# Full attention layers in runs of three score tiles, with one exponential tile of a quad on VectorE

## The chip, the cores and the metric

The kernel runs on one core of a Trainium2 chip. The metric is the device time of one execution in microseconds (us). The engines are named as in the profile: PE (TensorE, matmuls), PEld (its weight loads), DVE (VectorE), ACT (ScalarE), POOL (GpSimd) and SP (the engine whose queue issues the DMAs).

## The reference

Four transformer attention layers on one sequence of S = 2048 tokens and D = 512 features, with 32 heads of 16 features each. Layers 0 and 2 look back over a sliding window of 256 tokens, layers 1 and 3 attend to all 2048 tokens in both directions.

```python
q, k, v = split_heads(layernorm(x) @ wqkv)          # 32 heads of 16
scores = einsum("bhqd,bhkd->bhqk", q, k) * 16 ** -0.5
# layers 0, 2: positions outside 0 <= i - j < 256 are masked
p = softmax(scores)
x = x + merge_heads(einsum("bhqk,bhkd->bhqd", p, v)) @ wo
# x = x + A(x); x = x + B(x); x = x + A(x); x = x + B(x)   (A: window, B: full; weights shared)
```

In a full layer each head has 2048 x 2048 scores, all of which need an exponential.

## The kernel before

**Quads.** In a full layer the unit of work is a quad: four heads (two pairs) against one block of 512 queries. There are 8 quads of heads and 4 query blocks `c`, so 32 quads in a layer. Layer 1 goes through them block by block; layer 3 takes two quads of one feature tile `t` for each block in turn, 16 such blocks of two quads. A quad runs over 16 tiles `j` of 128 keys. For each `j` and each of the two pairs PE multiplies keys with queries (line 714, two matmuls of 64 rows side by side, one for each head) into a score tile of 128 keys by 2 x 512 queries in PSUM, and ACT writes its exponential to SBUF in float32 (line 718). So a quad has 32 score tiles and 32 exponentials. The values of one `j` are four float32 matmuls, one for each head (line 758; the profile shows two passes of each, eight records), which add up over the 16 `j` in the PSUM tile `acc[0]`, a quarter of the partitions for each head. A column of ones in the values adds up the denominator. Behind the last `j` the epilogue (lines 681 to 703) transposes `acc[0]` on DVE, divides by the denominator and writes the result as two float16 parts.

**PSUM.** In the full layers the eight banks hold `acc[0]`, `acc[1]` and three score tiles of two banks each: two of a rotating pool and `PH["third"]`. Every third score tile takes the third, so tile number k always uses the place of tile k - 3.

**Order on PE.** PE executes in the order in which the program is written; the other engines' orders are made by the framework from the priorities (`tc.high_priority(HEAD_START)` moves an instruction ahead). In `attn_full` one step is one `j`: both pairs' scores, then the values of the `j` two steps earlier (`pvq`, `flush(2)`), then side work.

**Side work** is everything that the neighbouring layers need: projections to queries, keys and values, the output projection and the layer norm behind it. It is cut into pieces of one matmul of 512 columns, which in full layers is issued as four matmuls of 32 columns abreast (`mms`, line 429), all into the bank `acc[1]`. A bank takes 12 pieces (3 in layer 3's output projection), and DVE then empties it; the planner lets 1.6 or 2.2 us of its own clock pass before it starts the next one (`PH["free"]`). `Side.share` hands out pieces against a budget; `Side.finish` issues what is left at the end of a stretch with no attention in between. `MM` is the planner's cost of one piece, 0.222 us.

**Loads.** `load_full` fetches a quad's queries (256 KB) and its keys in two halves (512 KB each) over SP's queue. There are three key buffers and two query buffers. The next quad's load is written at the start of the present one, but not over the end of a block.

Of the kernel before, what the change touches and what calls it, by code (L numbers as in the profile page):

```python
# [19 lines left out]
P = 128  # L20
# [13 lines left out]
EB, XB, XNB, WB, VB, OB = 6, 4, 4, 2, 3, 5  # L34
L_MIN = 2.0 ** -90
# [151 lines left out]
def fast_path(ctx, tc, flag, a_x, a_wqkv, a_wo, b_wqkv, b_wo, out):  # L187
# [20 lines left out]
    XC, XN, V, O, OT, KM, PH = {}, {}, {}, {}, {}, {}, {"free": 0.0}  # L208
    CM, DN, DC, WT, ST, pend = {}, {}, {}, {}, {}, []

# [287 lines left out]
    def project(l, s, c, act, ht=None, first=None):  # L498
# [14 lines left out]
        for t in range(NHT) if ht is None else (ht,):  # L513
# [9 lines left out]
            with tc.high_priority(HEAD_START):  # L523
# [33 lines left out]
    def keys(l, c, act, ht=None, first=None):  # L557
        sqs = yield from project(l, 1, c, act, ht, first)

        def rest():  # L560
# [4 lines left out]
            with tc.high_priority(HEAD_START):  # L565
                nc.vector.tensor_reduce(KM[l][r, c:c + 1], ph[r], axis=AX.X, op=ALU.max)  # L566
# [74 lines left out]
    def wo(l, c, tail):  # L641
# [4 lines left out]
        for i in range(4):  # L646
# [4 lines left out]
            with tc.high_priority(HEAD_START):  # L651
                nc.vector.tensor_tensor(d, ps, gcol[l % 2], ALU.mult)
# [25 lines left out]
    def epilogue(l, c, qd, a):  # L678
# [6 lines left out]
        with tc.high_priority(HEAD_START if l % 2 else 0):  # L685
            nc.vector.transpose(ot.rearrange("p b r -> p (b r)"), a)  # L686
# [19 lines left out]
    def exps(name, kt, qt, pr, pieces):  # L706

        turn["s"] += 1
        ps = PH["third"] if PH["full"] and turn["s"] % 3 == 0 else ps_s.tile([P, 2, QC], F32, name=f"s{name}", tag="s")
        w0 = min(p[3] for p in pieces)  # L710
        w1 = max(p[3] + p[2] for p in pieces)
# [5 lines left out]
        e = pp.tile([P, 2, QC], F32, name=f"e{name}", tag="e", bufs=EB)  # L717
        nc.scalar.activation(e[:, :, w0:w1], ps[:, :, w0:w1], AF.Exp, scale=SCALE)  # L718
        return e
# [30 lines left out]
    def attn_full(l, c, qd, kt, qt, a):  # L750
        for j in range(NT):
            es_ = []
            for pr in range(2):
                es_.append(exps(f"{l}_{c}_{qd}_{j}_{pr}", kt[j // 8], qt, pr, [(j % 8 * P, 0, QC, 0)]))

            def pv(j=j, es_=es_):
                for h in range(4):
                    nc.tensor.matmul(a[32 * h:32 * h + DH + 1, :], V[l, qd // 4, j // 8][:, j % 8, 4 * (qd % 4) + h, :],  # L758
                                     es_[h // 2][:, h % 2, :], start=(j == 0), stop=(j == NT - 1),
                                     skip_group_check=True)  # L760
            yield pv
# [5 lines left out]
    def attn_win(l, c, qd, kt, qt, a):  # L767
        first = True
        for u, tiles in enumerate(WTILES):
            tiles = [p for p in tiles if c or p[0] >= 0]  # L770
            es_ = []
            for pr in range(2):
# [4 lines left out]
                for b, far in edges:  # L777
                    v = ev[:, :, b, :]
                    with tc.high_priority(HEAD_START):
# [80 lines left out]
    class Side:  # L860

        def __init__(self, steps, works=(), following=(), least=0.0):
            self.next, self.least = list(following), least
            self.q, self.steps, self.cost, self.spent, self.k = [], steps, 0.0, 0.0, 0
            self.budget = self.lag = 0.0
# [10 lines left out]
        def one(self, force=False):  # L876

            if force:
                self.prefetch()
            at = [(w.ready_at(), i) for i, w in enumerate(self.q)]  # L880
# [11 lines left out]
        def piece(self, w):  # L892
# [4 lines left out]
            self.spent += abs(c)  # L897
            return c
# [9 lines left out]
        def step(self):  # L908
# [7 lines left out]
            if PH["full"]:  # L916
                return self.share()
# [6 lines left out]
        def share(self):  # L924

            self.budget = min(self.budget + max((self.cost - self.spent) / max(self.steps - 3 - self.k, 1), self.least), 0.75)
            self.lag = max(self.lag - max(0.29, self.least), -0.3)
            while self.q and clock[0] >= PH["free"] and self.budget >= MM / 2 and (self.lag < 0.25 or self.budget > 0.45):
# [4 lines left out]
                self.lag += abs(c)  # L933
# [21 lines left out]
    def attention(l, works):  # L955

        win = l % 2 == 0
        phase(l)
        load = load_win if win else load_full
        sd = None  # L960
        for t in range(NHT if l == 3 else 1):
            for c in range(NQ):
                qds = range(2 * t, 2 * t + 2) if l == 3 else range(NQD)
                if l == 1:

                    sd = sd or Side(NT * NQD // 2, works[0], works[1], 0.33)
                    while ("Q", 1, c) not in DONE:
                        sd.one(True)
                    settle()
                else:  # L970
                    sd = Side((3 if win else NT) * len(qds), works[t * NQ + c], works[t * NQ + c + 1], 0.34 if l == 3 and t < 2 else 0.0)
# [223 lines left out]
```

## Time and profile before

| | |
|---|---|
| median of 3 runs | 2768.49 us (2767.56 to 2770.2) |
| profiled execution | 2767.5 us, its span 2765.8 us |
| mean granted clock of PE | 0.992 |
| PE, ACT, DVE, POOL busy | 95%, 86%, 35%, 21% |
| layer 0 and what comes before it | 0 to 506 us |
| layer 1 (full) | 506 to 1458 us |
| layer 2 and its neighbours | 1458 to 1792 us |
| layer 3 (full) | 1792 to 2748 us |

The bounds of the layers are the first and last exponentials of each, as the trace has them. A row of the profile gives the line, the engine, the operation and its operands, then the count; matmuls are pipelined, so the length of one is more than the distance from one to the next. In the full layers ACT's instructions overlap too: one starts before the one ahead of it has ended, so distances between starts or ends tell more than durations.

### The profile page before, as it was taken

Reading aid. Unit: us, or ns where it says so; the run is one execution under the profiler, and the core shown is the slowest. Engines: PE = TensorE matmul, PEld = TensorE weight load, DVE = VectorE, ACT = ScalarE, POOL = GpSimd, SP = SyncE. Lnnn points to the kernel's source line nnn. Section 1 sums busy time; section 2 is a strip of 40 time slices with the busy share of each in tenths; the row PEclk is TensorE's granted clock in tenths of the full one; section 3 lists DMA queues with packets and bytes.
Section 4 is the critical chain, followed back from the end, with each engine's and each line's share of the span. In section 5 each row is a group of like instructions: output and inputs, shape, how many; then the busy total and the mean of one; then the engine's idle time right before and its main releaser. Section 6 shows DMA issues by size and latency. Waiting matters only on the chain.

```text
span 2765.8 us, 59954 instructions
## 1 busy us (share of the span) xinstructions
PE 2629.3 (95%) x24502; PEld 779.9 (28%) x24502; DVE 959.7 (35%) x2063; ACT 2377.9 (86%) x2683; POOL 567.7 (21%) x1129
## 2 busy tenths in 40 slices
PE   8989989999999999999998888899999999999997
PEld 4333334322222222222223333422222222222221
DVE  7678765112131113112215676512222222222122
ACT  3666655799999999999995677399999999999997
POOL 2577662000000000000005677100000000000000
PEclk9999999999999999999999999999999999999999
DMA  7877775422232123212325564623333343333331
GB/s 225 224 244 227 224 202 161 139 70 89 85 100 88 63 81 108 85 60 91 101 68 177 149 186 133 177 66 112 105 117 116 120 124 104 102 107 114 99 96 56
DMA packets 318542, 345.32 MB, mean 125 GB/s; under 512 B 113072, under 2 KB 234416, under 8 KB 312240
## 3 DMA queue, kind: packets, MB, share of 16 engines
q1 hardware_dynamic: 318256, 341.39, 41.0%
q8 instruction: 194, 3.18, 0.5%
q14 instruction: 92, 0.75, 0.1%
HBM read 228.59 MB, written 96.99 MB: 118 GB/s over the span
## 4 chain that ended last, share of the span: by engine, by line
PE 74%; ACT 8%; issue 6%; DVE 6%; POOL 3%; DMA 3%; SPq 0%; ACTq 0%; DVEq 0%; POOLq 0%
PE acc L758 30%; PE s L714 19%; PE acc L429 10%; PE b L432 9%; ACT e L718 7%; PE acc L791 3%; PE bs L432 1%; POOL e L781 1%; POOL e L784 1%; DVE ot L686 1%; POOL wr L344 1%; DMA w<-wd 1%; DVE xh L469 1%; DVE sp L528 0%; DVE xn L463 0%
## 5 line engine op out<-in xcount | busy, mean ns | idle before, releaser
L718 ACT ACTIVATE e<-s 128x1024 f32<-128x1024 f32 (+2 forms) x2432 | 2245.6, 1115 | 106.4 <-PE s L714 98.4
L758 PE MATMUL acc<-e,vt 128*17 128x512 f32 x8192 | 1078.8, 598 | 4.9 <-DVE ot L686 4.1
L714 PE MATMUL s<-qt,kt 64*128 64x512 f16 (+3 forms) x5504 | 777.8, 355 | 68.2 <-ACT e L718 40.0
L714 PEld LDWEIGHTS <-kt 64*128 64x128 f16 x5504 | 203.1, 94 | 807.4 <-issue 776.0
L784 POOL TENSOR_SCALAR_AFFINE_SELECT e<-e 128x256 f32<-128x256 f32 x512 | 230.4, 457 | 116.0 <-ACT e L718 115.3
L758 PEld LDWEIGHTS acc<-e,vt 128*17 128x17 f32 x8192 | 136.2, 95 | 383.6 <-issue 351.8
L686 DVE STREAM_TRANSPOSE ot<-acc 128x512 f32<-128x512 f32 x128 | 91.3, 714 | 374.6 <-PE acc L758 308.5
L781 POOL TENSOR_SCALAR_AFFINE_SELECT e<-e 128x256 f32<-128x256 f32 x448 | 196.8, 445 | 91.0 <-ACT e L718 89.5
L702 POOL TENSOR_TENSOR oh<-o,oh 128x512 f16<-128x512 f32 x31 | 36.0, 1161 | 860.2 <-DVE oh L701 860.2
L791 PE MATMUL acc<-e,vt 128*17 128x384 f32 (+2 forms) x2816 | 202.0, 393 | 6.1 <-POOL e L781 4.0
L432 PE MATMUL b<-xc,w 128*128 128x512 f16 x684 | 159.4, 384 | 16.8 <-DMA w<-wd 7.8
L533 POOL TENSOR_TENSOR sq_h<-sp_h 128x512 bf16<-128x512 f16 x27 | 28.1, 1041 | 510.8 <-DVE sp_h L527 510.8
L525 ACT ACTIVATE sp<-b,es 128x512 f16<-128x512 f32 x57 | 39.2, 688 | 96.0 <-PE b L432 93.7
L527 DVE TENSOR_SCALAR sp<-acc,es 128x512 f16<-128x512 f32 x28 | 20.9, 748 | 288.9 <-PE acc L429 288.9
L638 DVE COPY vt<-acc 128x256 f32<-128x256 f32 (+1 forms) x40 | 20.2, 504 | 288.9 <-PE acc L429 288.9
L527 DVE TENSOR_SCALAR sp_h<-acc,es 128x512 f16<-128x512 f32 x27 | 20.3, 751 | 277.8 <-PE acc L429 277.1
L533 POOL TENSOR_TENSOR sq<-sp 128x512 bf16<-128x512 f16 x28 | 29.1, 1041 | 396.9 <-DVE sp L527 396.9
L429 PE MATMUL acc<-xc,w_h 128*32 128x512 f16 x1296 | 108.1, 379 | 2.3 <-DVE km L566 2.3
L429 PE MATMUL acc<-xc,w 128*32 128x512 f16 x1344 | 108.9, 379 | 0.3
L673 DVE TENSOR_TENSOR dx<-acc,gcol 128x512 f32<-128x512 f32 x60 | 41.5, 692 | 176.7 <-PE acc L429 176.7
L429 PE MATMUL acc<-wv,xc 128*32 128x256 f16 (+1 forms) x1920 | 101.7, 306 | 0.0
L429 PE MATMUL acc<-wo,oh 128*32 128x512 f16 x1296 | 101.3, 379 | 0.0
(167 smaller groups left out, 1767.0 us busy)
## 6 DMA issues: line engine op xcount, KB each, us to landing
kt<-kf SPq DMA_DIRECT2D x128, 512.0 KB
qt<-qs SPq DMA_DIRECT2D x128, 256.0 KB
xd<-x SPq DMA_DIRECT2D x96, 256.0 KB
x<-xd SPq DMA_DIRECT2D x96, 256.0 KB
w<-wd SPq DMA_DIRECT2D x20, 1024.0 KB
kt<-kw SPq DMA_DIRECT2D x64, 256.0 KB
qs<-sp SPq DMA_DIRECT2D x48, 256.0 KB
wo<-wd SPq DMA_DIRECT2D x12, 1024.0 KB
```

The lines of the kernel that those rows point to most:

```text
L429: nc.tensor.matmul(ps[g:g + 32], a[:, g:g + 32], b, start=(i == 0), stop=(i == len(pairs) - 1), skip_group_check=True)
L432: nc.tensor.matmul(ps, a, b, start=(i == 0), stop=(i == len(pairs) - 1))
L527: nc.vector.tensor_scalar(sp[:, 0], ps, e, None, op0=ALU.mult)
L533: nc.gpsimd.tensor_tensor(sq, sp[:, 0], sp[:, 0], ALU.mult)
L673: nc.vector.tensor_tensor(d, ps, gcol[1], ALU.mult)
L686: nc.vector.transpose(ot.rearrange("p b r -> p (b r)"), a)
L714: nc.tensor.matmul(ps[:, h, s0:s0 + wd_], kt[R * h:R * h + R, pr, kc:kc + P], qt[R * h:R * h + R, pr, qc:qc + wd_], start=True, stop=True)
L718: nc.scalar.activation(e[:, :, w0:w1], ps[:, :, w0:w1], AF.Exp, scale=SCALE)
L758: nc.tensor.matmul(a[32 * h:32 * h + DH + 1, :], V[l, qd // 4, j // 8][:, j % 8, 4 * (qd % 4) + h, :], es_[h // 2][:, h % 2, :], start=(j ...
L781: nc.gpsimd.affine_select(v, v, pattern=[[0, 2], [-1, P]], compare_op=ALU.is_gt, fill=0.0, base=0, channel_multiplier=1)
L784: nc.gpsimd.affine_select(v, v, pattern=[[0, 2], [1, P]], compare_op=ALU.is_ge, fill=0.0, base=0, channel_multiplier=-1)
L791: nc.tensor.matmul(a[32 * h:32 * h + DH + 1, q * P:(q + nb) * P], V[l, (4 * c + j) // 4][:, j % 4, 4 * qd + h, :], es_[h // 2][:, h % 2, s ...
```

## The change

Only the full layers change; the window layers keep their step and merely get a function of their own (`attention_win`).

**Runs of three.** `attention_full` counts score tiles over quad ends. After every third one, `run` emits on PE: the values that became ready in earlier runs (at most two `j`, and none behind an epilogue), then side work. What became ready in this run waits for the next one. So PE's order is three score tiles, one to two `j`'s values, side pieces. The room for side pieces in a run is 1.79 us less 0.87 for each `j` emitted, and at least one piece (two behind an epilogue). The budget holds up to six pieces; a bank that was begun is filled before other work is taken (`within`).

**One exponential on DVE.** In all quads of layer 3 and those of layer 1's first three query blocks, the second pair's tile at `j` = 1 is not given to ACT. `exps_vector` reads the scores from PSUM with one DVE instruction over 2 x 512 columns, and then for each of the two heads computes the exponential in 10 instructions over 512 columns (round to a power of two, a polynomial of degree 6, scale). The result lies in a buffer of its own, `EX`, which takes one of the three places of the window layers' values; the work that needs the last place waits for the start of layer 1's last block (`"X"`). The values of `j` = 1 are issued in two halves: the first pair's with the others, the second pair's behind those of `j` = 12.

**Loads.** The next quad's keys and queries are requested after a run in the second half of a quad, as soon as what they need is done, also across blocks.

**Priorities.** Evictions that had a head start of 100 instructions get 300 in full layers (`head()`).

```diff
+JX, LATE = 1, 11
+    head = lambda: 3 * HEAD_START if PH["full"] else HEAD_START
...
+    def exps_vector(ps):
+        with tc.high_priority(head()):
+            nc.vector.tensor_scalar(EX[0][:, 0], ps, -126.0 / (SCALE * LOG2E), SCALE * LOG2E, op0=ALU.max, op1=ALU.mult)
+        b, k2 = EX[0][:, 1, 0], EX[0][:, 1, 1]
+        for h in range(2):
+            a = EX[0][:, 0, h]
+            nc.vector.tensor_scalar(k2, a, MAGIC, None, op0=ALU.add)
+            nc.vector.scalar_tensor_tensor(a, k2, MAGIC, a, op0=ALU.subtract, op1=ALU.subtract)
+            nc.vector.tensor_scalar(k2.bitcast(I32), k2.bitcast(I32), 23, None, op0=ALU.logical_shift_left)
+            nc.vector.tensor_scalar(b, a, POLY[6], POLY[5], op0=ALU.mult, op1=ALU.add)
+            nc.vector.tensor_tensor(b, b, a, ALU.mult)
+            for k in range(4, 0, -1):
+                nc.vector.scalar_tensor_tensor(b, b, POLY[k], a, op0=ALU.add, op1=ALU.mult)
+            nc.vector.scalar_tensor_tensor(a, b, POLY[0], k2, op0=ALU.add, op1=ALU.mult)
+        return EX[0][:, 0]
...
+        def emit(all_=False):
+            n, over = 0, False
+            while due:
+                f = due[0]
+                if f.__name__ == "pv":
+                    if not all_ and (n + f.size > 2 or over):
+                        break
+                    n += f.size
+                else:
+                    over = True
+                due.popleft()()
+            return n, over
+
+        def run():
+            nonlocal pairs, began
+            pairs = 0
+            spent(0.22)
+            n, over = emit()
+            due.extend(ready)
+            ready.clear()
+            sd.step(max(1.79 - 0.87 * n, 2 * MM if over else MM))
+            clock[0] = began = max(clock[0], began + 2.71)
...
+            vector = l == 3 or c < NQ - 1
...
+            for j in range(NT):
+                es_ = []
+                for pr in range(2):
...
+                    if vector and j == JX and pr:
+                        es_.append(exps_vector(scores(n, *piece)))
+                        ready.append(values_of(l, c, qd, j, es_, (0,)))
+                        held = values_of(l, c, qd, j, es_, (1,))
+                    else:
+                        es_.append(exps(n, *piece))
+                        if pr:
+                            ready.append(values_of(l, c, qd, j, es_))
+                    if pr:
+                        if vector and j == JX + LATE:
+                            ready.append(held)
+                        if j == NT - 1:
+                            ready.append(lambda c=c, qd=qd: epilogue(l, c, qd, acc[0]))
+                    pairs += 1
+                    if pairs == 3:
+                        run()
+                        if j >= NT // 2 and not ops and i + 1 < len(quads) and all(d in DONE for d in upcoming(i + 1)):
+                            settle(False)
+                            if not pend:
+                                ops = load_full(l, *quads[i + 1][1:])
```

167 lines of the change are left out of this document (99 added, 68 removed).

## The prediction

> **What bounds the kernel now.** I read the page first, then the two full layers (the parts of the change) by line, by wait and in order of time. The sum is made against the profiled execution: span 2765.8 us, its time 2767.5 us, 1.0 us under the median of 2768.49.
>
> ```profile
> span 2765.8 us, 59954 instructions
> PE 2629.3 (95%) x24502; PEld 779.9 (28%) x24502; DVE 959.7 (35%) x2063; ACT 2377.9 (86%) x2683; POOL 567.7 (21%) x1129
> PE 74%; ACT 8%; issue 6%; DVE 6%; POOL 3%; DMA 3%; SPq 0%; ACTq 0%; DVEq 0%; POOLq 0%
> ```
>
> The chain follows PE, but a busy PE is not a full one, so I asked how close ACT is to its own end in the full layers. Rows of the exponentials' line in layer 1 and in layer 3 (count, least/median/greatest ns, first and last start), and ACT alone in order of time (start, length, count):
>
> ```profile
> L718 ACT ACTIVATE e<-s x1024: 1017/1045/1590, 507.0 to 1456.8; 128x1024 f32<-128x1024 f32 x171
> L718 ACT ACTIVATE e<-s x1024: 1018/1124/1706, 1792.4 to 2745.8; 128x1024 f32<-128x1024 f32 x171
> 956.99 321.29 ACT L718 ACTIVATE e<-s 128x1024 f32<-128x1024 f32 x348 [0.28 <-PE s L714]
> 2499.62 247.93 ACT L718 ACTIVATE e<-s 128x1024 f32<-128x1024 f32 x270
> ```
>
> In the last row 270 tiles end within 247.93 us: (247.93 - 1.2 for the first)/269 = **0.917 us** a tile, with no gap; that is ACT's floor, although one tile takes 1.02 us from its start. A quad (32 tiles) can't go under 29.34 us there. Layer 1 takes 950.7 us (first start to last start and one tile), 29.7 a quad, layer 3 954.3, 29.8. Where side work is dense (third row) a tile takes 321.29/348 = 0.923. So both engines are near their limits, and all that a better order of PE can win is 0.4 us a quad.
>
> What PE does in a step of two tiles, dense (1004 to 1008) and nearly free of side work (2702 to 2704):
>
> ```profile
> 1004.73 1.05 PE L758 MATMUL acc<-e,vt 128*17 128x512 f32 x8
> 1005.60 0.61 PE L429 MATMUL acc<-xc,w 128*32 128x512 f16 x8
> 1006.14 0.61 PE L714 MATMUL s<-qt,kt 64*128 64x512 f16 x4
> 1006.68 1.05 PE L758 MATMUL acc<-e,vt 128*17 128x512 f32 x8
> 1007.55 0.40 PE L429 MATMUL acc<-xc,w 128*32 128x512 f16 x4
> 1007.88 0.61 PE L714 MATMUL s<-qt,kt 64*128 64x512 f16 x4
> ...
> 2002.68 0.38 PE L714 MATMUL s<-qt,kt 64*128 64x512 f16 x2
> 2002.99 1.05 PE L758 MATMUL acc<-e,vt 128*17 128x512 f32 x8
> ...
> 2702.98 1.05 PE L758 MATMUL acc<-e,vt 128*17 128x512 f32 x8
> 2703.96 0.92 PE L714 MATMUL s<-qt,kt 64*128 64x512 f16 x4
> ```
>
> From start to start: one tile's scores and the turn to the values 0.31 (2002.68 to 2002.99), two 0.54, so 0.23 for each tile ahead of the last; the values of one j 0.87; one side piece (four matmuls abreast) and the turn to the scores 0.33, two 0.54, so 0.21 for each further one; values straight to scores 0.98, that is 0.11 for the turn. A dense step is 0.54 + 0.87 + 0.33 or 0.54 = 1.74 or 1.95, on average 1.845 against ACT's 1.834: PE leads by a hair.
>
> How the two hand over:
>
> ```profile
> 506.50 0.66 ACT L636 ACTIVATE vt<-bs 128x256 f32<-128x256 f32 x2 [1.93 <-PE bs L432]
> 507.21 0.39 PE L714 MATMUL s<-qt,kt 64*128 64x512 f16 x2 [0.42 <-ACT vt L636]
> ...
> 2006.19 0.61 PE L714 MATMUL s<-qt,kt 64*128 64x512 f16 x4
> 2006.68 2.98 ACT L718 ACTIVATE e<-s 128x1024 f32<-128x1024 f32 x3 [1.42 <-PE s L714]
> ```
>
> A score matmul follows the end of the ACT operation that frees its bank by 0.05 us (507.16 to 507.21); an exponential follows its first score matmul by 0.49 (2006.19 to 2006.68).
>
> **The change, part by part.**
>
> *Runs of three.* There are three score buffers, and now PE writes all three in one go, then values, then side work. The third scores of a run (S3) need the third exponential of the run before to have ended. From S3's start the clock runs: that exponential ended 0.05 earlier and began 1.07 earlier; ACT took the run's first tile 0.917 after that, 0.15 before S3, and has work for 2.75 us, until S3 + 2.60. The next run's first scores must start 0.49 before that: **S3 + 2.10 us**. Now the step of two has 0.31 + 0.87 + 0.54 = 1.72 between its last scores and the next first ones, so it never meets this bound. In the run the distance depends on what it emits:
> - one j's values and four pieces: 0.31 + 0.87 + 0.33 + 3 x 0.21 = 2.14, 0.04 late;
> - two j's and one piece (the room given is at least one): 0.31 + 1.74 + 0.33 = 2.38, **0.28 late**; without a piece 0.31 + 1.74 + 0.11 = 2.16, 0.06 late.
>
> ACT can't earn this back: the run after a late one has PE early, but ACT still needs 2.75 for its three tiles. Three tiles make one j and a half, so one and two j's alternate; walking the queue of values through 32 quads by the code gives, for a quad, 4.3 runs with two j's, 2.0 with one and a half, 4.3 with one (5.3 and 5.3 without the vector tile). The saving is there too: three turns in 2.75 us in place of four and a half, some 0.1 a run of PE's time, but PE doesn't use it, since S3 waits.
>
> *The vector tile* (24 quads of layer 1, 32 of layer 3). ACT has 31 tiles, 28.43 us. But the j's values are cut in two halves, of two heads each. Is a half 0.44 or 0.87? The eight matmuls of a j (four heads, two passes) take 0.60 each and 1.05 together, so the four of a pass run abreast, and two would take as long:
>
> ```profile
> L758 PE MATMUL acc<-e,vt 128*17 128x512 f32 x4096 | 538.7, 598 | 3.8 <-DVE ot L686 3.2
> ```
>
> I take 0.87; the lower end is 0.44. Then both runs with one and a half j's, with the two pieces that they are given, are 0.31 + 1.74 + 0.54 = 2.59, 0.49 late (0.06 by the lower end). The vector tile's own run always has one j: in it ACT is done 0.92 early, at S3 + 1.18. With four pieces the next scores come at 2.14 all the same, so ACT idles through what it was spared; what remains is that the run of one and a half j's behind it isn't late on top. Without side work they come at 0.31 + 0.87 + 0.11 = 1.29, and 0.8 is won.
>
> A quad then: full of side work 29.34 + 4.3 x 0.28 + 0.49 = **31.0** (26 pieces); one piece a run 29.34 + 5.3 x 0.28 - 0.6 = 30.2 (11 pieces); none 29.34 + 5.3 x 0.06 - 0.8 = 28.9. Full and without a vector tile (layer 1's last eight) 29.34 + 5.3 x 0.28 = 30.8.
>
> *Side work.* Rows of the side matmuls in layer 1 (first four) and in layer 3:
>
> ```profile
> L429 PE MATMUL acc<-xc,w 128*32 128x512 f16 x1344 | 108.9, 379 | 0.3
> L429 PE MATMUL acc<-wo,oh 128*32 128x512 f16 x576 | 46.4, 379 | 0.0
> L429 PE MATMUL acc<-wv,xc 128*32 128x512 f16 x576 | 45.3, 379 | 0.0
> L429 PE MATMUL acc<-wv,xc 128*32 128x256 f16 x576 | 24.7, 273 | 0.0
> ...
> L429 PE MATMUL acc<-xc,w_h 128*32 128x512 f16 x1296 | 108.1, 379 | 2.3 <-DVE km L566 2.3
> L429 PE MATMUL acc<-wo,oh 128*32 128x512 f16 x720 | 54.9, 379 | 0.0
> L429 PE MATMUL acc<-wv,xc 128*32 128x256 f16 x768 | 31.7, 277 | 0.0
> ```
>
> By four, and the narrow ones by eight: 696 pieces in layer 1, 21.8 a quad; 600 in layer 3, 18.8. Between 30.2 and 31.0 that is 30.8 and 30.6; about one run in fourteen has none because a bank has just been filled (to 30.66 and 30.48). Layer 1: 32 x 30.66 = 981, **+30**. Layer 3: 32 x 30.48 = 975, **+21**. In layer 3's first half a block of two quads has 49 pieces and 21 runs at 2.2: walking its queue leaves two banks of the output projection for the forced end in seven blocks, six pieces (1.3 us) and one eviction between (1.2): 7 x 2.5 = **+17**, at least 0 if they fit.
>
> *Loads.* Keys and queries of the next quad are now issued in the second half of a quad, when their buffer is free, and over the ends of blocks. Stalls of this kind that cost PE now:
>
> ```profile
> PEld L714 <- DMA kt<-kf: 6.0, 1, 6.0
> ACT e L718 <- PE s L714: 13.5, 19, 6.0
> ```
>
> One, 6.0 us, at the head of layer 3, where nothing can be fetched ahead; of the other 7.5 us of ACT's waits there I take **-5** (0 to -7.5). SP's queue holds less behind a load that waits for its buffer; nothing on the path waits for that today.
>
> *DVE.* No 128x512 immediate operation stands in the trace; nearest rows:
>
> ```profile
> L653 DVE TENSOR_TENSOR x<-x,dx 128x512 f32<-128x512 f32 x12 | 8.8, 730 | 0.4
> L527 DVE TENSOR_SCALAR sp<-acc,es 128x512 f16<-128x512 f32 x28 | 20.9, 748 | 288.9 <-PE acc L429 288.9
> L463 DVE TENSOR_SCALAR xn<-x,mv,y 128x512 f32<-128x512 f32 x12 | 6.6, 548 | 0.3
> 1000.00:1050.00 50.00, 49.91 (x488) 11.68 (x488) 12.13 (x26) 49.93 (x55) 2.95 (x3) 1.00 0.27 91
> ```
>
> First operation on two banks at most 2 x 0.75 = 1.5, six with one input at 0.55, fourteen with two at 0.73: 15.0 us in one chain (13 if a one-input operation took half). It is wanted eight runs later, 8 x 2.8 = 22.4, in which DVE's other work (12.13 of 50) takes 5.4: 20.4, it fits. Evictions now wait up to one 0.7 us operation more; runs are 2.7 apart, so I take 0 for that, and up to +10.
>
> **Sum**: 2767.5 + 30 + 21 + 17 - 5 = 2830.5; **2830**. Lower ends: halves at 0.44 save about 0.4 in 56 quads, -22, no forced ends -17: 2791; upper: evictions +10, each run full +20: 2860. Likeliest case's own range 2791 to 2860.
>
> **The rivals.**
>
> *A, faster: the bound at S3 doesn't bind*, because the order in which PE's queue really runs lets the next first scores start under S3 + 2.10 in nearly all runs (it decides from 0.3 us a run). Then each engine runs at its own sum. PE, a quad: 10.67 x 0.77 + 17 x 0.87 + 21.8 x 0.21 + 10.67 x 0.12 = 28.9 in layer 1, 28.2 in layer 3; ACT 28.43. Layer 1: 24 x 28.9 + 8 x 29.34 = 928, -22; layer 3: 32 x 28.43 = 910, and some 8 of waits: -36. **2710**. For it: ACT's gapless 247.93 us; against it: three buffers and S3's place in the order. The Trainium skill (Perfetto Trace Analysis, Identifying the Most-Contended Engine) judges TensorE by its weight loads, not by its busy share, and takes the engine with the highest occupancy as the one to relieve: by that ACT bounds the full layers and PE, at 28% PEld, has room, so 56 tiles less would be 56 x 0.917 = 51 us off, near this case. The dense step of 1.845 against 1.834 speaks against it.
>
> *B, slower still: DVE is late.* If the chain interleaves with evictions and epilogues so that it ends 2 us behind its wanted run in a third of the quads, PE stands 18 x 2 = 37 us: **2867**. Against it: 20.4 of 22.4.
>
> *C, no change*: pieces fall mostly into the runs with one j, and the late runs just cancel what the vector tile spares: **2768**. Against it: the room is never under one piece.
>
> **How the numbers follow.** The forecast 0.52, A 0.33 (its partial forms with it), B 0.08, C 0.07. Range: 2710 to 2862 takes in A's upper half and B's lower edge and leaves out about 2 in 10. Faster by over 0.2% (5.5 us, about what a measurement here can tell from no change) 0.33, within 0.07, slower 0.60.
>
> **What would show it.** In the changed trace ACT would have a gap of 0.2 to 0.5 us behind most runs with two emissions of values, released by the scores; the third scores of a run would start 0.05 behind an ACT end; a half j's values would take 0.87. Layer 1 would last near 981 us and layer 3 near 987 with its ends. Wrong: if ACT's row stays unbroken at 0.917 a tile with 31 in a quad, or layer 1 is under 950 us.

## The result and the profile after

The change makes the kernel slower: **2917.38 us** in place of 2768.02 on the same chip, a ratio of **1.0539** (95% interval 1.0519 to 1.0559). The forecast was 2830, with 2862 as its upper end: the direction was right, and 87 us of the loss were missing.

The page of the changed kernel (span; busy time, share of the span and count of each engine; chain of waits by engine):

```profile
span 2911.3 us, 61028 instructions
PE 2656.0 (91%) x24502; PEld 875.1 (30%) x24502; DVE 1664.7 (57%) x3239; ACT 2355.0 (81%) x2627; POOL 577.6 (20%) x1129
PE 43%; ACT 14%; DVE 12%; issue 6%; DMA 1%; POOL 1%; SPq 0%; ACTq 0%; DVEq 0%
```

Before, PE held 74% of the chain and DVE 6%. Here the chain can be followed back only to 678 us (its shares add up to 77%), so the fair comparison is that stretch, 678 us to the end, in both kernels: PE had 78% of it and now has 56%, DVE had 54 us and now has 354, of which 224 are operations of the vector tile. So the chain now passes from PE to ACT and DVE and back. DVE's busy time grew by 705 us, while ACT was spared only 23 us. PE's busy time grew by 27 us with the same 24502 matmuls.

Where the time went, by stage, from the first to the last of the full layers' values matmuls in the trace: layer 1 949.5 to 1016.4 (+67), layer 3 951.9 to 1031.5 (+80), all between them 336.4 to 337.3. So the whole loss lies in the two full layers. ACT's exponentials there (count, busy, mean ns, idle time ahead of them and what ended it), first layer 1 and then layer 3 of the changed kernel:

```profile
L720 ACT ACTIVATE e<-s 128x1024 f32<-128x1024 f32 x1000 | 938.4, 1035 | 67.3 <-PE s L728 62.4 <-PE acc L784 4.5
...
L720 ACT ACTIVATE e<-s 128x1024 f32<-128x1024 f32 x992 | 933.1, 1033 | 106.9 <-PE s L728 88.4 <-PE acc L784 17.9
```

And the same two rows of the kernel before:

```profile
L718 ACT ACTIVATE e<-s 128x1024 f32<-128x1024 f32 x1024 | 947.1, 1084 | 3.7 <-PE s L714 2.7
...
L718 ACT ACTIVATE e<-s 128x1024 f32<-128x1024 f32 x1024 | 946.7, 1199 | 14.4 <-PE s L714 13.5
```

Idle time of 3.7 and 14.4 us has become 67.3 and 106.9. ACT now stands idle until score matmuls are there, and the score matmuls stand until ACT has freed a bank: each holds the other up. The waits of the whole run (waiter, releaser, us in total, times, longest):

```profile
ACT e L720 <- PE s L728: 246.1, 386, 15.0
PE s L728 <- ACT e L720: 131.3, 334, 1.4
PEld L558 <- DVE sp_h L536: 15.7, 12, 3.8
PE acc L437 <- DVE vt L646: 14.6, 14, 2.0
PE acc L437 <- DVE dx L681: 10.5, 17, 0.9
PE acc L558 <- POOL sq_h L541: 9.3, 6, 3.1
```

These sums hold the window layers too. In the two full layers alone the first row is 77.4 and 88.4 us (5.6 and 13.5 before), the second 44.7 and 46.5 (0.5 and 0.3 before). The last four rows are side work: matmuls that wait for a bank that DVE has not emptied, or for what GpSimd makes from it.

One pair of runs in order of time (start, length, count, idle time ahead):

```profile
991.78 0.82 PE L728 MATMUL s<-qt,kt 64*128 64x512 f16 x6
992.27 5.60 ACT L720 ACTIVATE e<-s 128x1024 f32<-128x1024 f32 x6 [0.98 <-PE s L728]
992.53 1.05 PE L784 MATMUL acc<-e,vt 128*17 128x512 f32 x8
993.40 1.04 PE L437 MATMUL acc<-xc,w 128*32 128x512 f16 x16
...
994.38 0.61 PE L728 MATMUL s<-qt,kt 64*128 64x512 f16 x4
995.18 0.39 PE L728 MATMUL s<-qt,kt 64*128 64x512 f16 x2 [0.19 <-ACT e L720]
995.50 1.91 PE L784 MATMUL acc<-e,vt 128*17 128x512 f32 x16
997.23 0.40 PE L437 MATMUL acc<-xc,w 128*32 128x512 f16 x4
997.56 0.61 PE L728 MATMUL s<-qt,kt 64*128 64x512 f16 x4
```

This is the bound of the forecast, S3 + 2.10 us. In the second run the third scores start at 995.18, released by ACT; two j's of values and one piece follow, and the next first scores start at 997.56, **2.38** later, the forecast's number. The pair takes 997.56 - 991.78 = 5.78 us for six tiles, where ACT's 0.917 would allow 5.50: 0.28 lost.

And one stretch that the forecast did not have (the same view, with DVE):

```profile
1995.16 0.65 DVE L746 SCALAR_TENSOR_TENSOR ex<-ex 128x512 f32<-128x512 f32 x1
1995.73 0.42 DVE L709 CAST oh<-o 128x512 f16<-128x512 f32 x1
1996.06 0.68 DVE L746 SCALAR_TENSOR_TENSOR ex<-ex 128x512 f32<-128x512 f32 x1
...
1996.66 0.42 DVE L646 COPY vt<-acc 128x256 f32<-128x256 f32 x1
...
1997.13 1.06 PE L437 MATMUL acc<-wv,xc 128*32 128x256 f16 x32 [1.41 <-DVE vt L646]
1998.12 0.82 PE L728 MATMUL s<-qt,kt 64*128 64x512 f16 x6
...
1998.61 1.94 ACT L720 ACTIVATE e<-s 128x1024 f32<-128x1024 f32 x2 [1.51 <-PE s L728]
```

PE stands 1.41 us until DVE has copied a full side bank. DVE is not idle: it works off operations of the vector tile (L746) and of the epilogue that stand ahead of the copy in its queue. The scores behind the side work come late, and ACT stands 1.51 us.

### The profile page after: what moved, and what is told of

Read it like the earlier page. It is cut to its first block, busy times and chain, and to the rows that moved or that the text cites. A ratio compares the mean times of both kernels' runs of the same rounds, so it can differ in the third digit from the quotient of the medians.

```text
span 2911.3 us, 61028 instructions
## 1 busy us (share of the span) xinstructions
PE 2656.0 (91%) x24502; PEld 875.1 (30%) x24502; DVE 1664.7 (57%) x3239; ACT 2355.0 (81%) x2627; POOL 577.6 (20%) x1129
## 4 chain that ended last, share of the span: by engine, by line
PE 43%; ACT 14%; DVE 12%; issue 6%; DMA 1%; POOL 1%; SPq 0%; ACTq 0%; DVEq 0%
PE acc L784 20%; ACT e L720 13%; PE s L728 12%; PE acc L437 5%; PE b L440 4%; DVE ex L746 3%; PE acc L817 1%; DVE ex L744 1%; DVE ex L736 1%; DVE ex L741 1%; DVE ot L694 1%; DVE ex L743 1%; DVE ex L742 1%; DVE ex L740 0%; DVE o L707 0%
## 5 line engine op out<-in xcount | busy, mean ns | idle before, releaser
L720 ACT ACTIVATE e<-s 128x1024 f32<-128x1024 f32 (+2 forms) x2376 | 2222.9, 1024 | 273.8 <-PE s L728 246.1
L784 PE MATMUL acc<-e,vt 128*17 128x512 f32 x7968 | 1028.7, 598 | 0.0
L728 PE MATMUL s<-qt,kt 64*128 64x512 f16 (+3 forms) x5504 | 763.7, 355 | 149.7 <-ACT e L720 131.3
L728 PEld LDWEIGHTS <-kt 64*128 64x128 f16 x5504 | 251.0, 94 | 804.9 <-issue 707.2
L746 DVE SCALAR_TENSOR_TENSOR ex<-ex 128x512 f32<-128x512 f32 x448 | 317.5, 709 | 10.5
L784 PEld LDWEIGHTS acc<-e,vt 128*17 128x17 f32 x7968 | 173.1, 96 | 412.0 <-issue 390.6
L710 POOL TENSOR_TENSOR oh<-o,oh 128x512 f16<-128x512 f32 x31 | 44.1, 1423 | 877.2 <-DVE oh L709 877.2
L736 DVE TENSOR_SCALAR ex<-s 128x1024 f32<-128x1024 f32 x56 | 68.1, 1217 | 251.7 <-PE s L728 251.7
L694 DVE STREAM_TRANSPOSE ot<-acc 128x512 f32<-128x512 f32 x128 | 91.1, 712 | 209.5 <-PE acc L784 143.9
L541 POOL TENSOR_TENSOR sq_h<-sp_h 128x512 bf16<-128x512 f16 x27 | 29.7, 1098 | 533.4 <-DVE sp_h L535 533.4
L541 POOL TENSOR_TENSOR sq<-sp 128x512 bf16<-128x512 f16 x28 | 31.4, 1121 | 477.1 <-DVE sp L535 477.1
L437 PE MATMUL acc<-wo,oh 128*32 128x512 f16 x1296 | 111.3, 380 | 14.0 <-DVE dx L681 10.5
L437 PE MATMUL acc<-wv,xc 128*32 128x256 f16 (+1 forms) x1920 | 101.5, 306 | 15.7 <-DVE vt L646 13.9
L440 PEld LDWEIGHTS <-w 128*128 128x128 f16 x720 | 67.9, 99 | 112.5 <-issue 35.6
```

Source lines behind the costliest of these rows:

```text
L437: nc.tensor.matmul(ps[g:g + 32], a[:, g:g + 32], b, start=(i == 0), stop=(i == len(pairs) - 1), skip_group_check=True)
L440: nc.tensor.matmul(ps, a, b, start=(i == 0), stop=(i == len(pairs) - 1))
L541: nc.gpsimd.tensor_tensor(sq, sp[:, 0], sp[:, 0], ALU.mult)
L728: nc.tensor.matmul(ps[:, h, s0:s0 + wd_], kt[R * h:R * h + R, pr, kc:kc + P], qt[R * h:R * h + R, pr, qc:qc + wd_], start=True, stop=True)
L736: nc.vector.tensor_scalar(EX[0][:, 0], ps, -126.0 / (SCALE * LOG2E), SCALE * LOG2E, op0=ALU.max, op1=ALU.mult)
L746: nc.vector.scalar_tensor_tensor(b, b, POLY[k], a, op0=ALU.add, op1=ALU.mult)
```

## The experiments

Quad times below are worked out from the starts of the values' matmuls, as the layer times above; "quads 5 to 24" are layer 1's middle, with side work in every run. All kernels ran beside the kernel before, whose medians lay between 2766.6 and 2768.3 us. Runs 8, 10, 13 and 15 are medians of 4 to 10 executions, the other runs a single one; executions of one kernel lay up to 12 us apart here (2763.82 to 2775.49).

**1. No vector tile, runs of three.** All 32 tiles of a quad go to ACT; the buffer of the vector tile is not taken.

```diff
-            vector = l == 3 or c < NQ - 1
+            vector = False
```

> Runs of three alone: all 32 exponentials of every quad on ACT, and no work waits for the vector tile's buffer. Theory S (the third scores' place in the run makes ACT wait, whatever DVE does): layer 1 near 983 us against 951 before, layer 3 near 1000 with its forced ends, the total 2846 (2832 to 2862). Rival D (the loss is DVE's: its chain delays evictions, and the order of PE is harmless): no more loss, 2745 to 2770.

Measured: **2897.94 us**. Layer 1's quads 5 to 24 take 30.93 us (forecast for a full quad without a vector tile: 30.8; before: 29.64). So the vector tile isn't the main cause: runs of three alone are 130 us slower than the kernel before, 52 more than the theory gave them. The middle of layer 1 fits; the excess is where side work is left over. Layer 1's last quad takes 49.8 us (28.4 before) and the quads of layer 3's first half 33.1 on average (30.3 before).

**2. Steps of two, values one step behind.** Three tiles a run become two, and side pieces are given out by the rule of before.

```diff
-                    if pairs == 3:
+                    if pairs == 2:
```

> The changed kernel with a run after every second score tile in place of every third, with the earlier rule for handing out side pieces; vector tile, halves, loads and priorities stay. Theory S: the third scores no longer wait, so most of the loss of the runs goes; what stays is the split values (0.87 a quad where side work is dense) and DVE's late evictions, 2815 (2795 to 2840). Rival D: the loss stays, 2890 or more.

Measured: **2958.14 us**, but the kernel doesn't test what it was made for. It emits the values of a step right behind the next step's scores, where the kernel before emits them two steps behind, and so the values on PE wait for the exponentials that they multiply (waits of layer 1):

```profile
PEld acc L784 <- ACT e L720: 20.2, 81, 0.5
```

That row is not among the waits of layer 1 before. Runs 5 and 6 put it right.

**3. Evictions with the head start.** The copies of L646 and the multiplications of L681 get the same head start in the planner as the other evictions.

```diff
-                    nc.vector.tensor_copy(to, fr)
+                    with tc.high_priority(head() if PH["full"] else 0):
+                        nc.vector.tensor_copy(to, fr)
```

> The changed kernel with the same head start for the two evictions of the side bank that have none (the copy to the values and the product with the output scale in layer 3). If they stand behind the vector tile's chain for want of a place in DVE's order, the waits of PE for them go: 2890 (2880 to 2900). If DVE is simply busy when they come, nothing changes: 2913 (2905 to 2922).

Measured: **2919.27 us**, no change. A head start in the planner doesn't help: by the count given at runs 12 and 13, 53 of 201 evictions still stand behind two or more chain operations, against 57 in the changed kernel.

**4. The vector tile's first operation only.** 20 of its 21 operations are left out, so what stands for its exponentials are scaled scores. The score bank is still freed by DVE, ACT is still spared a tile, the values are still cut in halves.

```diff
-            nc.vector.tensor_scalar(EX[0][:, 0], ps, -126.0 / (SCALE * LOG2E), SCALE * LOG2E, op0=ALU.max, op1=ALU.mult)
-        b, k2 = EX[0][:, 1, 0], EX[0][:, 1, 1]
...
-            nc.vector.scalar_tensor_tensor(a, b, POLY[0], k2, op0=ALU.add, op1=ALU.mult)
+            nc.vector.tensor_scalar(EX[0][:, 0], ps, 1.0, SCALE * LOG2E, op0=ALU.max, op1=ALU.mult)
```

> The changed kernel with only the first of the vector tile's 21 DVE instructions: it takes the greater of score and 1, scaled, in place of the exponential; the 20 others are left out, so DVE is busy 1.2 us a quad in place of 14. PE's and ACT's work is the same. Theory S with a part of DVE's: 2860 (2845 to 2870), the rest of the loss is PE's order. Rival D: at or under 2768.

Measured: **2868.48 us**. So the rest of the chain costs 2917.4 - 2868.5 = **49 us**, and the tile that ACT is spared wins 2897.9 - 2868.5 = 29 us on the way. The waits for evictions shrink (whole run, to be read beside 14.6 and 15.7 above):

```profile
PE acc L437 <- DVE vt L646: 2.4, 3, 0.8
...
PEld L558 <- DVE sp_h L536: 1.6, 5, 0.4
```

**5 and 6. Steps of two with values two steps behind**, with the vector tile in all 56 quads (5), and without one (6). Both also have run 2's edits.

```diff
             n, over = emit()
-            due.extend(ready)
+            due.extend(last)
+            last[:] = ready
             ready.clear()
```

> The changed kernel with its runs shortened from three tiles to two, side pieces given out as before the change, and the values of a step two steps behind its scores, as before the change. The vector tile stays in all 56 quads, with its values cut in two halves, and the loads stay as changed. Nothing of the computation is left out. Theory (the run of three is what costs most, because its third scores stand 2.1 us ahead of the next first ones, and a vector tile costs its chain's delay of evictions on top): the bound of the run goes, the chain stays. A dense step is led by TensorE by 0.01 us, so the extra half of a j's values (0.87) in 40 dense quads is paid in full less the 0.17 that 1.845 lies near ACT's 1.834 over 16 steps: 0.7 x 40 = 28; in 16 quads with little side work ACT's 0.917 is won, -14; evictions behind the chain +45; loads -4: 2767 + 55 = 2822 us (2795 to 2845). Rival A (in steps of two the vector tile pays as ACT's count says): 56 x 0.917 = 51 off, about 2715. Rival (something else of the rewrite costs): 2880 or more.

> As the kernel of steps of two with values two steps behind, but with no vector tile and no buffer for one: all 32 tiles of a quad on ACT. Nothing is left out. Theory (run of three costs about 130 us by itself: the kernel of runs of three without a vector tile took 2898): only the loads' order and small parts of the rewrite stay, 2764 us (2752 to 2776). Rival (the loss of 130 us lies in other parts of the rewrite, such as the order in which side pieces are taken or the loads issued ahead): 2850 to 2900.

Measured: run 6 **2766.78 us** beside 2766.89 of the kernel before. The rest of the rewrite (loads ahead, order of side pieces) costs nothing that can be told, and the whole 131 us between run 1 and run 6 belong to the run of three and what it does to side work. Run 5: **2885.88 us**, 64 more than expected: in steps of two the vector tile costs 119 us, against 19 in runs of three (2917.4 - 2897.9). Its time lies in the range of the rival, but run 6 rules out the rival's cause, something else of the rewrite. ACT's rows of layer 1, run 6 and then run 5:

```profile
L720 ACT ACTIVATE e<-s 128x1024 f32<-128x1024 f32 x1024 | 946.8, 1069 | 2.6 <-PE s L728 1.9
```

```profile
L720 ACT ACTIVATE e<-s 128x1024 f32<-128x1024 f32 x1000 | 933.9, 1041 | 60.1 <-PE s L728 58.9
```

24 tiles fewer, and 57 us more idle time: what ACT is spared (24 x 0.917 = 22 us), it waits away more than twice over.

**7. No side piece where two j's are emitted.** As run 1, but a run with two j's has no side work.

```diff
-            sd.step(max(1.79 - 0.87 * n, 2 * MM if over else MM))
+            sd.step(0.0 if n == 2 else 1.79 - 0.87 * n)
```

> Runs of three without a vector tile (the kernel that took 2897.9), and now a run that emits two j's values gets no side piece, while a run with one j keeps four. Nothing is left out, side work only moves. Theory (a run is late where its third scores stand over 2.10 us ahead of the next first ones): two j's without a piece are 2.16, 0.06 late in place of 0.28, so a quad in the middle of layer 1 takes 29.34 + 5.3 x 0.06 + 5.3 x 0.04 = 29.9 us in place of 31.0. Room for side pieces falls from 26.7 to 21.3 a quad where 21.8 are needed, so more of them is left for the ends of blocks: the whole 2860 to 2900. Rival (the time per run has another cause, such as the length of PE's own work): PE's work per quad is the same, quads stay at 30.9 to 31.1 and the ends come on top: 2910 or more.

Measured: **2930.03 us**. The quads of layer 1 do what the bound says: quads 5 to 24 take **29.87** (expected 29.9; the rival 30.9 or more). ACT's row in order of time is whole over 14 tiles:

```profile
999.41 13.06 ACT L720 ACTIVATE e<-s 128x1024 f32<-128x1024 f32 x14
```

PE in the same stretch goes from three tiles' scores to two j's of values, to scores, to one j and four pieces, with no wait:

```profile
1000.80 0.98 PE L728 MATMUL s<-qt,kt 64*128 64x512 f16 x6
1001.71 1.91 PE L784 MATMUL acc<-e,vt 128*17 128x512 f32 x16
1003.56 1.03 PE L728 MATMUL s<-qt,kt 64*128 64x512 f16 x6
1004.52 1.05 PE L784 MATMUL acc<-e,vt 128*17 128x512 f32 x8
1005.39 1.05 PE L437 MATMUL acc<-wv,xc 128*32 128x512 f16 x16
```

The whole missed: expected 2860 to 2900. The side pieces that found no room came at the ends: layer 1's last quad takes 69.5 us, and layer 3's first half 36.0 a quad. A part of the excess may be PE's clock: the granted clock of this one execution was 0.978 (0.95 from 1850 to 2400 us, where run 1 had 0.99), and the two were not separated. A run of three either pays 0.28 for a piece beside two j's, or pays later for not having placed it.

**8. Steps of two, a vector tile only where side work is sparse** (the 16 quads of layer 3's second half).

```diff
-            vector = l == 3 or c < NQ - 1
+            vector = l == 3 and t >= 2
```

> Steps of two with values two steps behind, and a vector tile only in the second half of layer 3 (16 quads), where side work is sparse and ACT's row was unbroken before the change. Nothing is left out. Theory (where PE has room, a tile taken from ACT is won in full): 29.3 us a quad there become 28.4 to 28.6, 16 x 0.8 = 13 off, and 4 off for the loads: 2750 us (2742 to 2762). Rival (evictions behind DVE's chain cost there as well, some 0.8 us a quad): 2762 to 2775, no gain that can be told.

Measured: **2784.49 us**, ratio 1.0066 (1.0049 to 1.0083): 18 us lost where 13 were to be won. Those quads take 30.50 instead of 29.24. In order of time, at a quad's turn:

```profile
2555.68 1.22 DVE L736 TENSOR_SCALAR ex<-s 128x1024 f32<-128x1024 f32 x1
...
2556.82 0.70 DVE L694 STREAM_TRANSPOSE ot<-acc 128x512 f32<-128x512 f32 x1
...
2557.58 1.05 PE L784 MATMUL acc<-e,vt 128*17 128x512 f32 x8 [1.21 <-DVE ot L694]
```

The vector tile is the second j's. Its 1.22 us operation stands ahead of the transpose that frees the accumulator for the new quad, and PE waits 1.21.

**9 and 10. The tile at the fifth j, and its values whole.** Run 9 moves the tile away from the turn; run 10 also emits both pairs of its j together at the fifteenth.

```diff
-JX, LATE = 1, 11
+JX, LATE = 4, 10
...
-                        ready.append(values_of(l, c, qd, j, es_, (0,)))
-                        held = values_of(l, c, qd, j, es_, (1,))
+                        held = values_of(l, c, qd, j, es_)
```

> The kernel of steps of two with a vector tile only in the second half of layer 3 (2784.5 us), with the vector tile moved from the second j of a quad to the fifth, and its second values from the thirteenth to the fifteenth. Nothing is left out. Theory (at the second j the 1.22 us first operation of the vector tile stands on VectorE ahead of the 0.70 us transpose that frees the accumulator for the new quad, and PE waits 1.2 us where it waited some 0.4): 0.8 x 16 quads come back, 2784.5 - 13 = 2771 us (2764 to 2777). Rival (the turn is not what costs, it is the evictions of side work behind the chain): 2780 to 2787.

> As that kernel with the vector tile at the fifth j, and the values of that j are not cut in two halves: both pairs wait and are emitted as one whole j at the fifteenth, with a buffer of its own for the ACT tile that waits. Nothing is left out. Theory (a half j takes PE 0.87, as much as a whole one, and in these quads PE and ACT are even): 16 x 0.87 = 14 at most come off PE, so 29.2 us a quad become 28.5 to 29.0, and the whole 2757 us (2748 to 2767). Rival (PE is not what bounds these quads): no better than with two halves.

Measured: run 9 **2783.34 us**, no change, though the wait at the turn is gone (these quads' weight loads behind L694 wait 0.8 us at most). Those quads still take 30.57: other waits came in its place. PE's waits for the transpose fall there from 5.0 us in all to 1.2, but the waits for L681's evictions rise from 5.8 to 9.4 and those for GpSimd's squares of side work (L541) from 3.8 to 6.6. So the turn was a wait that could be seen, but not what set the time; the time lies in the rival's range. Run 10 **2778.31 us** (1.0037; 1.0025 to 1.0050): a whole j in place of two halves may win about 5 us, not 14, and not enough.

**11. Steps of two, the vector tile's first operation only**, in all 56 quads (the edit of run 4 on run 5).

> The kernel of steps of two with the vector tile in all 56 quads (2885.9 us), with 20 of the tile's 21 operations on VectorE left out: what stands for its exponentials is the scaled scores, so the output is not the reference's. Theory (the chain's delay of the evictions costs as much as in runs of three, 49 us or 0.85 a quad, and the rest is the half j's 0.87 on a PE that leads, and the turn of the accumulator): 2837 us (2825 to 2850). Rival A (in steps of two the chain is nearly all of it): 2770 to 2800. Rival B (the chain costs little there): 2865 to 2886.

Measured: **2803.65 us**. Here the chain costs 2885.9 - 2803.7 = **82 us**, and all that is left of the vector tile 37. Neither the expected size nor a rival: closest to "nearly all of it".

**12 and 13. The chain given out in small groups**: three operations a run in the changed kernel (12), two a step in run 10's kernel (13).

```diff
+            chain_on(3)
             clock[0] = began = max(clock[0], began + 2.71)
```

> The changed kernel with the same 21 operations of the vector tile, but given out three a run behind the run's side work, so that VectorE's queue holds them in small groups with the evictions of side banks between them; before, all 21 stood in the order at once. Nothing is left out. Theory (an eviction stands behind two to six operations of the chain that started after its bank was full, in 81 of 265 evictions, and that is what the chain costs): most of the 49 us between the changed kernel and the one without the chain comes back, 2872 us (2862 to 2885). Rival A (the chain costs by its length on VectorE, wherever it stands): 2905 to 2920. Rival B (the spread chain ends behind the run that wants its values): over 2930, with waits of the values for VectorE.

> Steps of two, a vector tile in the 16 quads of layer 3's second half, its j's values whole (2778.3 us), and the chain given out two operations a step. Nothing is left out. Theory (what is left against 2766.8 is evictions behind the chain, and without them ACT's spared tile shows): 2778 - 16 x 0.9 = 2763 us (2756 to 2770). Rival (the order of the chain isn't what costs there): 2774 to 2780.

Measured: **2916.97** and **2778.17 us**, no change, and no test either: the planner put the operations as early as before. From its first operation's start to its last one's end a chain takes 16.2 us (median) in the changed kernel and 16.4 in run 12. An eviction here is the first DVE operation that reads a full side bank, 201 in the two full layers. For each I counted the chain operations that start between the end of the last side matmul ahead of it and its own start. In the changed kernel there are two to six for 57 of the 201, in run 12 for 50. (The 81 of 265 in the expectation come from another way of counting.)

**14 and 15. The groups held back by a dependence.** One operation of each group takes its constant from a one-column tile that GpSimd makes from the run's last exponentials, so the group can't stand far ahead.

```diff
+        nc.gpsimd.tensor_scalar(g, e[:, 0, 0:1], 0.0, v, op0=ALU.mult, op1=ALU.add)
...
-            nc.vector.tensor_scalar(k2, a, MAGIC, None, op0=ALU.add)
+            nc.vector.tensor_scalar(k2, a, gated(MAGIC), None, op0=ALU.add)
```

> The changed kernel with the chain given out three operations a run, and each such group now really held back: one operation of it takes its constant from a small tile that GpSimd makes from that run's last exponential tile, so the group can't start before that tile is there. (Given out three a run without this, the chain stood in VectorE's queue as before, and the time was the same, 2917 us.) Nothing is left out. Theory (evictions stand behind several operations of the chain): now at most about three stand ahead of one instead of six, so a third to a half of the 49 us comes back: 2890 us (2880 to 2903). Rival A (the chain costs by its length, wherever it stands): 2910 to 2922. Rival B (an eviction stands behind a group that itself still waits, so the queue costs more): over 2922.

> Steps of two, the vector tile in 16 quads of layer 3 with whole j's, two chain operations a step, each pair held back in the same way. Nothing is left out. Theory (the order in VectorE's queue is what is left of the cost): 2778 less about half of 16 x 0.9, 2771 us (2764 to 2775). Rival A (length, not order): 2776 to 2781. Rival B (the queue blocks more): over 2781.

Measured: run 14 **2879.87 us**: 37.5 of the chain's 49 us come back with the same operations, more than the third to a half expected. Now 11 of the 201 evictions stand behind two chain operations and none behind more; the mean time from a full bank to its eviction's start falls from 0.86 to 0.57 us (0.06 in the kernel before, 0.11 in run 4). PE's waits for DVE and GpSimd in the full layers, 53.6 us in the changed kernel and 15.3 in run 4, are 28.1. Two groups in DVE's queue, each held back until GpSimd's tile is there, and a copy of a side bank (L646) that gets in between the operations of one:

```profile
977.52 0.49 DVE L756 TENSOR_SCALAR ex<-ex,g 128x512 f32<-128x512 f32 x1 [1.62 <-POOL g L739]
...
980.53 0.75 DVE L761 SCALAR_TENSOR_TENSOR ex<-ex,g 128x512 f32<-128x512 f32 x1 [1.07 <-POOL g L739]
981.20 0.69 DVE L646 COPY vt<-acc 128x512 f32<-128x512 f32 x1
981.80 1.41 DVE L761 SCALAR_TENSOR_TENSOR ex<-ex 128x512 f32<-128x512 f32 x2
```

So most of the chain's cost is its place in the queue, not its length. Run 15: **2770.15 us**, ratio 1.0008 (0.9998 to 1.0019): no change against the kernel before. The vector tile's cost is smaller, but not gone: its 16 quads take 29.69 us, against 30.50 in run 8, 30.21 in run 10 and 29.24 in run 6 and in the kernel before. ACT is spared 16 x 0.917 = 14.7 us there, but its idle time in these quads rises from 0.7 us in run 6 to 18.0. The rest of the rewrite makes up for most of it: layer 1 takes 947.3 us in run 15 as in run 6 (949.5 before), a quad of layer 3's first half 30.0 (30.25 before). None of these kernels beats the one before.

## Why the prediction was right or wrong

The loss can be told by parts, each the difference of two runs. Rewrite without its two ideas: 0 (run 6). Runs of three: +131 (run 1 against 6). ACT's spared tile, less its half j: -29 (run 4 against 1). The chain: +49 (changed kernel against run 4), 37 to 38 of it by its place in the queue (run 14). These differences must add up, to +151 against run 6, since each starts where the last one ends; the prices hold for this order of parts (in steps of two the chain costs 82).

**The bound at S3 + 2.10** was right, and so was its price. The distances are in the trace as forecast: in layer 1 of the changed kernel (640 to 1440 us) the median from S3 to the next first scores is 2.38 for two j's and a piece (98 runs; 2.38 forecast) and 2.16 for one j and four pieces (79 runs; 2.14). Layer 1's full quads without a vector tile take 30.93 against 30.8, and run 7 takes them to 29.87 by keeping the pieces out. With the vector tile and no chain (run 4) they take 30.80 against 31.0. Rival A, that the order lets this bound go, falls: ACT's row has 67 us of holes in layer 1. Rival C falls with it.

**A half j takes 0.87**: the traces agree. In the same stretch the distance is 2.57 for one and a half j's and two pieces (29 runs; 2.59 forecast), and 2.36 for one and a half j's and one piece (7 runs), beside 2.38 for two whole j's and one piece. In layer 1 of run 11 a step with a half j alone and one piece takes 1.72 us, hardly less than one with a whole j, 1.74. A half j in layer 3 of the changed kernel:

```profile
1991.70 1.47 PE L784 MATMUL acc<-e,vt 128*17 128x512 f32 x10
1992.59 0.39 PE L437 MATMUL acc<-wv,xc 128*32 128x256 f16 x4
1993.01 0.60 PE L784 MATMUL acc<-e,vt 128*17 128x512 f32 x2
1993.43 0.39 PE L437 MATMUL acc<-wv,xc 128*32 128x256 f16 x4
1993.75 0.99 PE L728 MATMUL s<-qt,kt 64*128 64x512 f16 x6
```

The first row is a whole j and the half j's first pass, two matmuls that start at 1992.58; its second pass starts at 1993.01. Four of the eight side matmuls start beside the first pass, but the others start only at 1993.43, 0.85 behind it.

**The step that failed is the price of DVE's chain.** I took 0 for the delay of the evictions (up to +10), because one operation of 0.7 us fits between runs 2.7 apart. That counts one operation in progress. But DVE's order is made when the program is built, and in it two to six chain operations stand ahead of 57 of the 201 evictions although the bank is full (the mean wait of a full bank is 0.86 us, without the chain 0.11). That such a bank fills earlier than the planner thought is my reading; no run tested it. Measured: 49 us. The chain's length was no problem, as I had said: 13.8 us a quad by its rows against my 15.0 at most, and in all 56 quads it ends at least 6.8 us before the values that want it. So rival B (the values wait for a late chain) was wrong as well: DVE was late, but to another customer.

**The left-over side work was under-sized**, by some 38 us with the smaller parts; this or the chain's 49 alone would have put the time above my range. I had +17 for forced ends in layer 3 and nothing at the end of layer 1. There, one work of four banks finds no room among the runs (PE, changed kernel):

```profile
1506.17 1.91 PE L784 MATMUL acc<-e,vt 128*17 128x512 f32 x16
...
1509.17 2.77 PE L437 MATMUL acc<-wv,xc 128*32 128x512 f16 x48 [0.54 <-DVE km L574]
1512.73 2.77 PE L437 MATMUL acc<-wv,xc 128*32 128x512 f16 x48 [0.79 <-DVE vt L646]
...
1522.45 1.91 PE L784 MATMUL acc<-e,vt 128*17 128x512 f32 x16
```

From 1509 to 1522 PE does side work alone, and ACT stands 15 us. Layer 1's last quad takes 40.7 us, some 10 more than forecast. Run 4, which has no chain, shows the rest: layer 3's first half takes 32.5 a quad, 31.0 and 24 us of ends by my own quad price, against the +17; its second half 30.25, where one piece a run was priced at 30.2. In all run 4 is 38 us over the forecast: some 10 at layer 1's end, 6 in its other quads (30.86 against 30.66), 19 in layer 3 (52 against 21 + 17 - 5), and 3 outside these. With the chain's 49 that is the 87. The -5 for the loads shows in the full layers of run 6, which has the new loads: 947.3 and 948.4 us against 949.5 and 951.9. Its whole time, 2766.78 us beside 2766.89, doesn't show it.

**The tile that ACT is spared** is worth 29 us in runs of three (run 4), some of it through less left-over work, since the last quad of layer 1 falls from 49.8 to 40.7. In steps of two it is a loss of 37 even without the chain (run 11). PE's waits for the transpose at the turn are part of it, 15.5 us against 3.8 in run 6. The rest fits a half j that PE has to pay, since PE leads the dense step by a hair, as the forecast read from the kernel before; no run takes the two apart. The rule of the Trainium skill (Perfetto Trace Analysis, Identifying the Most-Contended Engine), by which ACT was the engine to relieve, gave 51 us off; no run here shows that, the nearest are the 29 of run 4 and the loss of 37 of run 11. Here the two engines' times for a dense step are within 1% of each other (1.845 us against 1.834), which their shares of busy time, 95% and 86%, don't tell.

What stays open: what the 11 us of the chain's cost are that run 14 doesn't bring back, how much of run 11's 37 us is the half j, and what would have to go for ACT's idle time in run 15 to fall below what it is spared.

## What to carry to other kernels

When two engines hand buffers to each other, work out the longest time that one may take between its last request and its next first one, and check every step of the order against it: a longer run with the same average work can break this bound in every second step. Work moved to an engine with idle time isn't free if that engine also empties banks; count the operations that may stand ahead of an eviction, not the one in progress. And room for side work is a budget over the stage: what finds none comes at the end, where nothing covers it.

## What the runs showed that I had not expected

- The order in which operations are given out hardly moves them in DVE's queue: neither a head start for evictions (2919.27 us) nor giving the chain out three a run (2916.97) changed the time, and in the latter the chain stayed as long, 16.4 us against 16.2. A dependence through a one-column tile did both (2879.87 us; 22.1 us for a chain).
- The same chain costs 49 us in runs of three and 82 in steps of two. One reading is that in runs of three part of it falls where PE waits for ACT anyway; it was not tested.
- DVE's 128x512 f32 operations on SBUF took 0.42 to 0.45 us with one input and 0.69 to 0.75 with two, the two-bank one from PSUM 1.22, so the chain was 13.8 us where the nearest rows of before had given 15.0.
